# Layer scale on one core: 32-row pieces in six shared slots, all loads queued ahead of all stores on the two hardware rings

## The chip, the cores and the metric

One Trainium2 chip (trn2), one core. The time is device microseconds of one execution; the span is the time from the first to the last instruction in its profile. "Before" ran at 123.72 us (median of 3, from 123.56 to 123.85). I call a difference real only where several rounds and their interval show it.

## The reference

```python
B, S, D = 1024, 16, 512          # x, y: (B, S, D) bf16, gamma: (D,) bf16
def reference(x, y, gamma):
    return x + gamma * y
```

Two inputs and one output of 16.78 MB each must cross between DRAM and SBUF: 50.33 MB in all. There is one multiply and one add per element, and no reuse.

## The kernel before

The 16,384 rows of 512 elements are dealt to 128 partitions, so each partition owns 128 consecutive rows, 128 KB. A "piece" of n rows is n KB per partition; one transfer moves it for all partitions.

```python
MAIN_CHUNK = 16
TAIL_CHUNKS = [8, 8]
X_BUFS = 5
Y_BUFS = 6
# ... chunks = seven pieces of 16 rows, then 8 and 8
# ... pad_sb: unused bytes, so that the tiles begin at a multiple of 16,384 bytes
x_pool = ctx.enter_context(tc.tile_pool(name="xio", bufs=X_BUFS))
y_pool = ctx.enter_context(tc.tile_pool(name="yio", bufs=Y_BUFS))
# ... gamma is spread over the partitions by a matmul with a row of ones
r0 = 0
for cs in chunks:
    xt = x_pool.tile([P, max_chunk, D], xf.dtype, tag="xt")
    yt = y_pool.tile([P, max_chunk, D], yf.dtype, tag="yt")
    nc.sync.dma_start(out=xt[:, :cs, :], in_=xv[:, r0 : r0 + cs, :])      # hardware ring of SP
    nc.scalar.dma_start(out=yt[:, :cs, :], in_=yv[:, r0 : r0 + cs, :])    # hardware ring of ACT
    nc.vector.tensor_tensor(out=yt, in0=yt, in1=gamma_sb[:, None, :].to_broadcast(...), op=mult)  # cut
    nc.vector.tensor_tensor(out=yt, in0=xt, in1=yt, op=add)                                       # cut
    nc.gpsimd.dma_start(out=ov[:, r0 : r0 + cs, :], in_=yt[:, :cs, :])    # software queue of POOL
    r0 += cs
```

Stores are issued as soon as a piece is added, so they run beside the loads of later pieces.

## Time and profile before

| | before |
|---|---|
| time, median | 123.72 us |
| span of the profiled execution | 122.05 us |
| VectorE busy | 71.1 us, 58% |
| bytes | 33.56 MB read, 16.78 MB written |
| first DMA packet starts, last one ends | 1.73 us, 120.47 us |

The page of the kernel before, cut to the rows that matter: busy time by engine, then the span in 40 slices (busy tenths of VectorE and of the 16 DMA engines, and what they moved), then the DMA queues (q1 is SP's ring and carries x, q10 is ACT's and carries y, q0 is the software queue of POOL and carries the stores).

```profile
span 122.0 us, 123 instructions
...
PE 0.6 (0%) x1; PEld 0.1 (0%) x1; DVE 71.1 (58%) x21; POOL 5.6 (5%) x14
...
DVE  0010799780019999950079995940019999859600
...
DMA  4999999999999999999999999999999999999993
GB/s 118 424 435 430 430 430 430 430 349 435 430 430 435 435 440 430 430 430 430 430 440 435 430 430 430 430 430 430 430 397 454 413 430 419 464 430 430 397 427 126
...
q10 hardware_dynamic: 1296, 16.78, 32.7%
q1 hardware_dynamic: 1296, 16.78, 32.7%
q0 software_dynamic: 1328, 16.78, 32.2%
```

The DMA row is 9 in all but the first and last slice, and each of the three queues takes a third of the engines' time. The kernel is bound by the DMA engines; the zeros of VectorE cost nothing. One slice, near 26 us, moved only 349 GB/s although the engines were busy in it.

The groups of instructions of the same profile (busy us and mean ns of one, then the idle time before them and what ended it):

```profile
L94 DVE TENSOR_TENSOR yt<-yt,gamma_sb 128x8192 bf16<-128x8192 bf16 (+1 forms) x9 | 35.5, 3949 | 35.5 <-DMA yt<-in_y_dram 35.5
L100 DVE TENSOR_TENSOR yt<-xt,yt 128x8192 bf16<-128x8192 bf16 (+1 forms) x9 | 35.2, 3944 | 0.0
```

The last part of its timeline (start us, us, engine, line, operation):

```profile
108.26 2.29 DVE L94 TENSOR_TENSOR yt<-yt,gamma_sb 128x4096 bf16<-128x4096 bf16 x1 [2.02 <-DMA yt<-in_y_dram]
110.47 4.49 DVE L100 TENSOR_TENSOR yt<-xt,yt 128x4096 bf16<-128x4096 bf16 x2
113.05 0.53 POOL L106 DMA_DIRECT2D out_dram<-yt  x1 [8.18 <-DVE yt L100]
115.25 0.53 POOL L106 DMA_DIRECT2D out_dram<-yt  x1 [1.67 <-DVE yt L100]
```

The last y lands at 108.2 us. After that come two short multiplies, two short adds and two 1 MB stores; the 8-row tail is there so that this end is short.

 16 KB in 611 ns on 16 engines is 429 GB/s. The Trainium skill, page "DMA: Bandwidth & Descriptors", section "Where 436 GB/s comes from", puts the ceiling of the ports at 435 GB/s for the 16 engines; the trace agrees to 1.5%, so nothing that leaves the bytes alone can win more than a little. The same section says that for transfers between HBM and SBUF a limit of about 358 GB/s per core binds; the 429 GB/s here, with one core at work, lie above it, so here the measurement decides.

### The profile page before, as it was taken

How to read it: one execution, taken by the hardware profiler on the slowest of the kernel's cores; microseconds unless marked ns; L12 is line 12 of the kernel's file. 1: busy time of each engine (PE TensorE's matmuls, PEld its weight loads, DVE VectorE, ACT ScalarE, POOL GpSimd, SP SyncE). 2: the span in 40 equal slices, each digit the busy share in tenths (PEclk: the TensorE clock that was granted, in tenths of full speed). 3: DMA queues.
4: the chain of work that ended last, by engine and by line, in shares of the span. 5: the costliest groups of instructions: out<-in, count | busy, mean ns of one | idle time of the engine just before them, and what ended most of it. 6: DMA issues, size and time to landing. Idle time of an engine off the chain costs nothing.

```text
span 122.0 us, 123 instructions
## 1 busy us (share of the span) xinstructions
PE 0.6 (0%) x1; PEld 0.1 (0%) x1; DVE 71.1 (58%) x21; POOL 5.6 (5%) x14
## 2 busy tenths in 40 slices
PE   0010000000000000000000000000000000000000
PEld 0000000000000000000000000000000000000000
DVE  0010799780019999950079995940019999859600
POOL 2000000100000010100000011000000010100300
DMA  4999999999999999999999999999999999999993
GB/s 118 424 435 430 430 430 430 430 349 435 430 430 435 435 440 430 430 430 430 430 440 435 430 430 430 430 430 430 430 397 454 413 430 419 464 430 430 397 427 126
DMA packets 3920, 50.33 MB, mean 412 GB/s; under 512 B 464, under 2 KB 464, under 8 KB 464
## 3 DMA queue, kind: packets, MB, share of 16 engines
q10 hardware_dynamic: 1296, 16.78, 32.7%
q1 hardware_dynamic: 1296, 16.78, 32.7%
q0 software_dynamic: 1328, 16.78, 32.2%
HBM read 33.56 MB, written 16.78 MB: 412 GB/s over the span
## 4 chain that ended last, share of the span: by engine, by line
DMA 66%; issue 15%; DVE 11%; POOL 1%; POOLq 0%; DVEq 0%; ACTq 0%
DMA yt<-in_y_dram 50%; DMA out_dram<-yt 16%; DVE yt L100 7%; DVE yt L94 4%; POOL out_dram L106 1%; POOLq L134 0%; DVEq L94 0%; POOLq L106 0%; ACTq L93 0%; DVEq L100 0%
## 5 line engine op out<-in xcount | busy, mean ns | idle before, releaser
L94 DVE TENSOR_TENSOR yt<-yt,gamma_sb 128x8192 bf16<-128x8192 bf16 (+1 forms) x9 | 35.5, 3949 | 35.5 <-DMA yt<-in_y_dram 35.5
L100 DVE TENSOR_TENSOR yt<-xt,yt 128x8192 bf16<-128x8192 bf16 (+1 forms) x9 | 35.2, 3944 | 0.0
L106 POOL DMA_DIRECT2D out_dram<-yt x9 | 4.8, 533 | 109.1 <-DVE yt L100 109.1
L86 DVE CAST gamma_sb<-gamma_ps 128x512 bf16<-128x512 f32 x1 | 0.7, 690 | 7.5 <-PE gamma_ps L85 7.5
L80 POOL DMA_DIRECT2D gamma_row<-in_gamma_dram x1 | 0.6, 618 | 0.8 <-POOLq L123 0.8
L81 DVE MEMSET ones_row<- 1x128 bf16 x1 | 0.2, 165 | 0.8 <-PEq L123 0.8
L85 PE MATMUL gamma_ps<-gamma_row,ones_row 1*128 1x512 bf16 x1 | 0.6, 577 | 7.9 <-DMA gamma_row<-in_gamma_dram 7.9
L123 POOL MEMSET const-float32-0.0<- 128x1 f32 x1 | 0.1, 98 | 0.2 <-issue 0.2
L123 POOL MEMSET const-bfloat16-1.0<- 128x1 bf16 x1 | 0.1, 102 | 0.0
L85 PEld LDWEIGHTS <-ones_row 1*128 1x128 bf16 x1 | 0.1, 101 | 1.0 <-DVE pad_sb L83 1.0
L123 POOL MEMSET const-float32-1.0<- 128x1 f32 x1 | 0.1, 98 | 0.0
L123 POOL MEMSET const-uint8-127<- 128x1 uint8 x1 | 0.1, 98 | 0.0
L83 DVE MEMSET pad_sb<- 128x16 uint32 x1 | 0.1, 72 | 0.0
## 6 DMA issues: line engine op xcount, KB each, us to landing
yt<-in_y_dram ACTq DMA_DIRECT2D x7, 2048.0 KB, 45.5
xt<-in_x_dram SPq DMA_DIRECT2D x7, 2048.0 KB, 45.4
out_dram<-yt POOLq DMA_DIRECT2D x7, 2048.0 KB, 19.1
xt<-in_x_dram SPq DMA_DIRECT2D x2, 1024.0 KB, 44.4
yt<-in_y_dram ACTq DMA_DIRECT2D x2, 1024.0 KB, 32.7
out_dram<-yt POOLq DMA_DIRECT2D x2, 1024.0 KB, 5.5
gamma_row<-in_gamma_dram POOLq DMA_DIRECT2D x1, 1.0 KB, 6.6
```

The lines of the kernel that those rows point to most:

```text
L80: nc.gpsimd.dma_start(out=gamma_row[:], in_=gamma.unsqueeze(0))
L81: nc.vector.memset(ones_row[:], 1.0)
L83: nc.vector.memset(pad_sb[:, 0:64], 0)
L85: nc.tensor.matmul(gamma_ps[:], ones_row[:], gamma_row[:], start=True, stop=True)
L86: nc.vector.tensor_copy(out=gamma_sb[:], in_=gamma_ps[:])
L94: nc.vector.tensor_tensor(out=yt[:, :cs, :], in0=yt[:, :cs, :], in1=gamma_sb[:, None, :].to_broadcast([P, cs, D]), op=mybir.AluOpType.mult,)
L100: nc.vector.tensor_tensor(out=yt[:, :cs, :], in0=xt[:, :cs, :], in1=yt[:, :cs, :], op=mybir.AluOpType.add,)
L106: nc.gpsimd.dma_start(out=ov[:, r0 : r0 + cs, :], in_=yt[:, :cs, :])
L123: nc = _bacc.Bacc("TRN2", target_bir_lowering=False, num_devices=1)
```

## The change

The intent: longer transfers (half as many packets), no software queue in the way, and no store that delays a load. The schedule is fixed by hand, in program order. The diff, cut to its core (gone with it: the tail, the pad, the two pools):

```diff
-MAIN_CHUNK = 16
-TAIL_CHUNKS = [8, 8]
-X_BUFS = 5
-Y_BUFS = 6
+PIECE = 32
+SLOTS = 6
 ...
+    io_pool = ctx.enter_context(tc.tile_pool(name="io", bufs=SLOTS))
+    xs, ys = [], []
+    ctx.enter_context(tc.manual_schedule())
+    for c in range(n_pieces):                      # 4 pieces
+        r = slice(c * PIECE, (c + 1) * PIECE)
+        xt = io_pool.tile([P, PIECE, D], dt, tag="io")
+        yt = io_pool.tile([P, PIECE, D], dt, tag="io")
+        nc.sync.dma_start(out=xt[:], in_=xv[:, r, :])
+        nc.scalar.dma_start(out=yt[:], in_=yv[:, r, :])
         nc.vector.tensor_tensor(... mult ...)
         nc.vector.tensor_tensor(... add ...)
-        nc.gpsimd.dma_start(out=ov[:, r0 : r0 + cs, :], in_=yt[:, :cs, :])
+        xs.append(xt)
+        ys.append(yt)
+    for c in range(n_pieces):
+        r = slice(c * PIECE, (c + 1) * PIECE)
+        eng = nc.sync if c % 2 == 0 else nc.scalar
+        eng.dma_start(out=ov[:, r, :], in_=ys[c][:])
```

Eight tiles share six slots. In the built program x3 takes the slot of x0 (it waits for the first add) and y3 that of x1 (it waits for the second).

More of the change, by code (lines that the diff above doesn't have):

```diff
@@ L6 @@
 from concourse._compat import with_exitstack
-MAIN_CHUNK = 16
-TAIL_CHUNKS = [8, 8]
-X_BUFS = 5
-Y_BUFS = 6
-SBUF_ALIGN = 16384
-SLOT_ROUND = 32
-def _chunk_schedule(n_per_part: int) -> list[int]:
-    tail = [c for c in TAIL_CHUNKS if c < MAIN_CHUNK]
-    rem = n_per_part - sum(tail)
-    if rem < 0:
-        return [1] * n_per_part
-    chunks = []
-    while rem >= MAIN_CHUNK:
-        chunks.append(MAIN_CHUNK)
-        rem -= MAIN_CHUNK
-    if rem > 0:
-        chunks.append(rem)
-    chunks.extend(tail)
-    assert sum(chunks) == n_per_part, (chunks, n_per_part)
-    return chunks
-def _round_up(v: int, m: int) -> int:
-    return ((v + m - 1) // m) * m
+PIECE = 32
+SLOTS = 6
 @with_exitstack
@@ L51 @@
     N, D = xf.shape
-    assert N % P == 0, (N, P)
-    n_per_part = N // P
-    gdt = gamma.dtype
+    rows = N // P
+    n_pieces = rows // PIECE
+    dt = xf.dtype
     xv = xf.rearrange("(p n) d -> p n d", p=P)
@@ L58 @@
     ov = of.rearrange("(p n) d -> p n d", p=P)
-    chunks = _chunk_schedule(n_per_part)
-    max_chunk = max(chunks)
     const_pool = ctx.enter_context(tc.tile_pool(name="const", bufs=1))
-    gamma_row = const_pool.tile([1, D], gdt)
-    ones_row = const_pool.tile([1, P], gdt)
-    gamma_sb = const_pool.tile([P, D], gdt)
-    used = nc.sbuf_base
-    used = _round_up(used, SLOT_ROUND)
-    for nbytes in (D * mybir.dt.size(gdt), P * mybir.dt.size(gdt), D * mybir.dt.size(gdt)):
-        used += _round_up(nbytes, SLOT_ROUND)
-    pad_bytes = (-used) % SBUF_ALIGN
-    pad_sb = None
-    if pad_bytes > 0:
-        pad_sb = const_pool.tile([P, pad_bytes], mybir.dt.uint8)
-    x_pool = ctx.enter_context(tc.tile_pool(name="xio", bufs=X_BUFS))
-    y_pool = ctx.enter_context(tc.tile_pool(name="yio", bufs=Y_BUFS))
+    gamma_row = const_pool.tile([1, D], dt)
+    ones_row = const_pool.tile([1, P], dt)
+    gamma_sb = const_pool.tile([P, D], dt)
     psum_pool = ctx.enter_context(tc.tile_pool(name="psum", bufs=1, space=bass.MemoryType.PSUM))
@@ L81 @@
     nc.vector.memset(ones_row[:], 1.0)
-    if pad_sb is not None:
-        nc.vector.memset(pad_sb[:, 0:64], 0)
     gamma_ps = psum_pool.tile([P, D], mybir.dt.float32)
@@ L86 @@
     nc.vector.tensor_copy(out=gamma_sb[:], in_=gamma_ps[:])
-    r0 = 0
-    for cs in chunks:
-        xt = x_pool.tile([P, max_chunk, D], xf.dtype, tag="xt")
-        yt = y_pool.tile([P, max_chunk, D], yf.dtype, tag="yt")
-        nc.sync.dma_start(out=xt[:, :cs, :], in_=xv[:, r0 : r0 + cs, :])
-        nc.scalar.dma_start(out=yt[:, :cs, :], in_=yv[:, r0 : r0 + cs, :])
+    io_pool = ctx.enter_context(tc.tile_pool(name="io", bufs=SLOTS))
[7 more added lines that the diff above has]
+        nc.scalar.dma_start(out=yt[:], in_=yv[:, r, :])
         nc.vector.tensor_tensor(
-            out=yt[:, :cs, :],
-            in0=yt[:, :cs, :],
-            in1=gamma_sb[:, None, :].to_broadcast([P, cs, D]),
+            out=yt[:],
+            in0=yt[:],
+            in1=gamma_sb[:, None, :].to_broadcast([P, PIECE, D]),
             op=mybir.AluOpType.mult,
         )
-        nc.vector.tensor_tensor(
-            out=yt[:, :cs, :],
-            in0=xt[:, :cs, :],
-            in1=yt[:, :cs, :],
-            op=mybir.AluOpType.add,
-        )
-        nc.gpsimd.dma_start(out=ov[:, r0 : r0 + cs, :], in_=yt[:, :cs, :])
-        r0 += cs
-    assert r0 == n_per_part
+        nc.vector.tensor_tensor(out=yt[:], in0=xt[:], in1=yt[:], op=mybir.AluOpType.add)
+        xs.append(xt)
[4 more added lines that the diff above has]
+        eng.dma_start(out=ov[:, r, :], in_=ys[c][:])
 _INS = ['x', 'y', 'gamma']
```

## The prediction

> What bounds it now. 50.33 MB move (the page: 33.56 read, 16.78 written) and the 16 DMA engines are never free: the row of DMA busy tenths is 9 in every slice but the first and last, at 430 to 435 GB/s in most. VectorE is 58% busy and waits 35.5 us for y (groups by line): off the critical path. In the packet records a 16 KB packet takes 611 ns and an 8 KB packet 309, load or store, mixed or alone: 604 ns of data per 16 KB and 7 fixed, 429 GB/s on 16 engines, close to the 435 GB/s ceiling in the Trainium skill, "DMA: Bandwidth & Descriptors", section "Where 436 GB/s comes from". Between the first packet (1.73 us) and the end of the last (120.47) the mean engine is without one for 0.62 us. Each engine has 168 long and 48 short data packets, 117.5 us, and 28 completion packets of 9 ns. So of the span of 122.05 us, 1.7 are start, 117.7 packets, about 1.0 slow packets (one slice falls to 349 GB/s), skew and gaps, 1.6 the end.
>
> What the change does. Bytes stay. Packets become longer: at 32 KB 96 per engine x 1215 ns (estimate, 2 x 604 + 7) = 116.6 us; if still cut at 16 KB, 192 x 611 = 117.3. Completion packets: 13. Stores leave the software queue, whose stores land with up to 1.4 us between the first and last of 16 engines; the first eight hardware loads show 0.5 or less. The pad goes: tiles begin at byte 18,816, not a multiple of 256.
>
> Does an engine run dry? VectorE from its two shapes: 151 ns + 0.5215 per element, so 8.70 us at 16,384, 17.45 a pair. x0, y0 land near 22.6 us (second pair of before: 22.7), later pairs 19.4 apart: 42, 61.5, 81. Adds end near 40, 59.5, 79, 98.5. In the built program x3 waits for the first add and y3 for the second, so both are queued by 59.5, before x2 and y2 end at 61. Stores 0 and 1 run 80 to 100; store 2 is queued at 79, store 3 at 98.5, 1.5 us before it is wanted; the other ring would fill a short gap. VectorE stays hidden, with about 2 us of slack, and the first add at 40 instead of 22 us costs nothing because loads fill that time.
>
> Sum: start 1.7 + packets 116.7 to 117.4 + residue 0.5 + end 1.5 = 120.4 to 121.1 us of span, 1.0 to 1.6 less; the timed run is 1.67 above the span: 122.1 to 122.8. I say 122.4.
>
> Right if: DMA tenths stay 9; loads to 80 us, then stores alone near 430 GB/s; VectorE 70 us busy, TENSOR_TENSOR near 8.7; x3, y3 issued near 40 and 59.5; last landing near 119.5; stores' landing spread about 0.5.
>
> Wrong if: 40 us of stores alone run slower than the 12 us of them at the end of before (over 124); tiles off 256-byte alignment cost DMA beats (same page, "How a descriptor splits into AXI transactions": an unaligned start fetches unused bytes; I take under 1%, no run shows it yet); the slack is lost and both rings go empty; the end shrinks more than I think (towards 121).
>
> Chances: faster by over 2% 0.08, within 2% 0.85, slower by over 2% 0.07. Range 121.5 to 123.7.

## More of the kernel before

The trace also has a record of every DMA packet (start, duration, size, queue). A packet here is what one partition contributes to one transfer. Durations are remarkably constant:

```
packet      median duration     in which kernel
 8 KB         309 ns            before (tail)
16 KB         611 ns            before, loads and stores alike
32 KB        1213 ns            after, loads and stores alike
```

So a packet costs 301 to 302 ns per 8 KB plus 7 to 9 ns that do not depend on its size.

## The result, and the profile after

| | before | after |
|---|---|---|
| median | 123.67 us (4 runs, 123.56 to 123.85) | 123.22 us (4 runs, 123.17 to 123.34) |
| ratio | | 0.9964, 95% interval 0.995 to 0.9978 |

A ratio is the mean time of one kernel's fast runs over that of the other's fast runs in the same rounds, so it is not quite the ratio of the medians that stand beside it. A second set of five rounds (after_again below) gave 0.9966. The change is real and small: 0.45 us, where I had announced 1.3.

The page of the changed kernel, the same rows:

```profile
span 121.5 us, 80 instructions
...
PE 0.6 (0%) x1; PEld 0.1 (0%) x1; DVE 70.4 (58%) x10; POOL 0.8 (1%) x5
...
DVE  0002000499999399999679999907999990000000
...
DMA  5899999999999999999999999989898989898992
GB/s 173 378 486 389 475 399 464 399 464 421 442 432 432 410 453 410 453 399 464 410 453 410 453 410 453 345 345 518 356 507 356 507 356 507 367 496 389 475 410 108
...
q10 hardware_dynamic: 864, 25.17, 48.7%
q1 hardware_dynamic: 864, 25.17, 48.6%
q0 software_dynamic: 32, 0.00, 0.0%
```

Bytes and packets are counted in the slice in which a packet starts. With packets of 1.2 us in slices of 3 us the numbers swing (345, then 518): two neighbours have to be averaged. The pair 345, 345 near 77 us does not average out; that is a true loss.

Its groups and the timeline of its VectorE and rings:

```profile
L58 DVE TENSOR_TENSOR yt<-yt,gamma_sb 128x16384 bf16<-128x16384 bf16 x4 | 34.8, 8692 | 18.9 <-DMA yt<-in_y_dram 18.9
L64 DVE TENSOR_TENSOR yt<-xt,yt 128x16384 bf16<-128x16384 bf16 x4 | 34.8, 8692 | 0.1
```

```profile
0.74 59.20 ACTq L57 DMA_DIRECT2D yt<-in_y_dram  x4
0.74 39.83 SPq L56 DMA_DIRECT2D xt<-in_x_dram  x4
...
22.80 8.69 DVE L58 TENSOR_TENSOR yt<-yt,gamma_sb 128x16384 bf16<-128x16384 bf16 x1 [11.05 <-DMA yt<-in_y_dram]
31.52 8.69 DVE L64 TENSOR_TENSOR yt<-xt,yt 128x16384 bf16<-128x16384 bf16 x1
40.61 38.78 SPq L70 DMA_DIRECT2D out_dram<-yt  x2
...
82.85 8.69 DVE L58 TENSOR_TENSOR yt<-yt,gamma_sb 128x16384 bf16<-128x16384 bf16 x1 [3.83 <-DMA yt<-in_y_dram]
91.57 8.69 DVE L64 TENSOR_TENSOR yt<-xt,yt 128x16384 bf16<-128x16384 bf16 x1
```

The first add ends at 40.2 us, the last load lands at 82.8 us instead of 108.2, the last add ends at 100.3 us, and from there VectorE has nothing to do while 20 us of stores are still queued. The schedule is the one predicted, to within 2 us.

Here is where the loss can be seen without packet records. Stretches of both kernels: their length, then busy us of the engines, the granted clock, the mean busy share of the DMA engines (which can pass 1, as a packet counts where it starts), and GB/s. First before, then after:

```profile
20.00:30.00 10.00, 0.00 (x0) 0.00 (x0) 6.37 (x2) 0.55 (x1) 1.00 1.01 408
30.00:75.00 45.00, 0.00 (x0) 0.00 (x0) 30.52 (x7) 1.59 (x3) 1.00 1.01 431
75.00:82.00 7.00, 0.00 (x0) 0.00 (x0) 4.43 (x1) 0.53 (x1) 1.00 0.98 419
```

```profile
20.00:30.00 10.00, 0.00 (x0) 0.00 (x0) 7.20 (x1) 0.00 (x0) 1.00 0.97 419
30.00:75.00 45.00, 0.00 (x0) 0.00 (x0) 40.93 (x6) 0.00 (x0) 1.00 1.00 431
75.00:82.00 7.00, 0.00 (x0) 0.00 (x0) 4.02 (x1) 0.00 (x0) 1.00 0.99 379
```

Two things are to be seen. In the long middle both kernels move 431 GB/s: the packets twice as long do not show. And after, between 75 and 82 us, the engines are as busy as ever (0.99) and move only 379 GB/s. Before has its slow stretch earlier (408 from 20 to 30 us).

### One sum for all kernels

From the packet records the time between the start of the first packet and the end of the last (the window) can be split without remainder:

window = nominal + slow + idle - overlap,

all in us per DMA engine. *Nominal* gives every packet the median duration of its size. *Slow* is what packets took beyond that. *Idle* is the time with fewer than 16 packets in flight, *overlap* that with more than 16 (an engine then has two packets in flight, and a part of one hides behind the other). A transfer has *landed* when all 16 engines have reported their part of it.

| | window | nominal | slow | idle | overlap | last landing to end | span |
|---|---|---|---|---|---|---|---|
| before | 118.74 | 117.74 | 1.26 | 0.62 | 0.89 | 1.23 | 122.05 |
| after | 118.20 | 116.58 | 1.55 | 0.44 | 0.37 | 1.14 | 121.45 |
| after_again | 118.24 | 116.58 | 1.51 | 0.54 | 0.38 | 1.15 | 121.48 |
| half_packets | 118.72 | 117.55 | 1.47 | 0.51 | 0.81 | 0.88 | 121.70 |
| pieces16 | 118.28 | 117.55 | 1.12 | 0.40 | 0.79 | 0.89 | 121.45 |
| before_no_tail | 119.22 | 117.55 | 1.40 | 1.09 | 0.82 | 1.18 | 122.47 |

(The first packet starts at 1.73 to 1.77 us in all of them; 0.34 to 0.52 us pass between the last packet's end and its landing. One line is one execution. Nominal and overlap follow the number of packets and repeat to 0.01 us between after and after_again; slow and idle scatter, so differences of 0.2 us in them mean little.) The change did remove 1.16 us of nominal packet time. It gave back 0.52 of overlap and 0.29 of slow packets, and won 0.18 of idle time: 0.54 us of window.

All but 0.05 us (before) and 0.18 us (after) of the slow time lies in two places. In the first 5 us each engine's first packet takes longer, up to 2.07 us instead of 1.21 in the changed kernel: 0.59 us per engine are lost before, 0.60 after. The second place comes just ahead of the first store, in packets of loads. Start, end, queue, ns and bytes of four of the 16 packets concerned, all of them y3 loads, and last the first packet of store 0:

```
77.636 79.650 q10 2014 32768
77.637 79.691 q10 2054 32768
77.677 79.670 q10 1993 32768
77.696 79.663 q10 1967 32768
...
80.767 81.980 q1 1213 32768
```

### The profile page after: what moved, and what is told of

Its sections match the earlier page's. It is cut to its first block, busy times and chain, and to the rows that moved or that the text cites. A ratio compares the mean times of both kernels' runs of the same rounds, so it can differ in the third digit from the quotient of the medians.

```text
span 121.5 us, 80 instructions
## 1 busy us (share of the span) xinstructions
PE 0.6 (0%) x1; PEld 0.1 (0%) x1; DVE 70.4 (58%) x10; POOL 0.8 (1%) x5
## 3 DMA queue, kind: packets, MB, share of 16 engines
q10 hardware_dynamic: 864, 25.17, 48.7%
q1 hardware_dynamic: 864, 25.17, 48.6%
## 4 chain that ended last, share of the span: by engine, by line
DMA 53%; DVE 29%; ACTq 0%; issue 0%
DMA yt<-in_y_dram 53%; DVE yt L58 14%; DVE yt L64 14%; ACTq L57 0%
## 5 line engine op out<-in xcount | busy, mean ns | idle before, releaser
L58 DVE TENSOR_TENSOR yt<-yt,gamma_sb 128x16384 bf16<-128x16384 bf16 x4 | 34.8, 8692 | 18.9 <-DMA yt<-in_y_dram 18.9
L64 DVE TENSOR_TENSOR yt<-xt,yt 128x16384 bf16<-128x16384 bf16 x4 | 34.8, 8692 | 0.1
```

The lines of the kernel that those rows point to most:

```text
L58: nc.vector.tensor_tensor(out=yt[:], in0=yt[:], in1=gamma_sb[:, None, :].to_broadcast([P, PIECE, D]), op=mybir.AluOpType.mult,)
L64: nc.vector.tensor_tensor(out=yt[:], in0=xt[:], in1=yt[:], op=mybir.AluOpType.add)
```

## The experiments

Theories at the start. **P**: as predicted, packets are paid one after the other, each with its fixed few ns, and the rest is the software queue's. **O**: half of the fixed part was already hidden by overlap, which I put down to packets of two queues. **W** (A in the expectations): the loss ahead of the first store is a one-time cost of an engine's first write, to this output (A1) or at all (A2). All kernels gave the reference's result.

| run | median us | ratio to before | 95% interval |
|---|---|---|---|
| warm_out | 123.29 | 0.9956 | 0.9939 to 0.9972 |
| warm_scratch | 123.28 | 0.9962 | 0.9947 to 0.9978 |
| half_packets | 123.28 | 0.9959 | 0.9944 to 0.9975 |
| tail_split | 123.29 | 0.9961 | 0.9948 to 0.9975 |
| before_last_hw | 123.68 | 1.000 | 0.9988 to 1.0013 |
| last_sw | 123.25 | 0.9965 | 0.9952 to 0.9977 |
| pieces16 | 123.21 | 0.9954 | 0.9939 to 0.9968 |
| after_again | 123.31 | 0.9966 | 0.9953 to 0.9979 |
| before_no_tail | 124.22 | 1.0038 | 1.0026 to 1.0051 |
| pieces16_sw | 127.84 | 1.0335 | 1.032 to 1.0349 |
| hw_mixed | 133.98 | 1.0834 | 1.082 to 1.0849 |
| sw_stores | 134.50 | 1.0897 | 1.0851 to 1.0943 |

### Packet length: half_packets and pieces16

half_packets, on the changed kernel:

```diff
-        nc.sync.dma_start(out=xt[:], in_=xv[:, r, :])
-        nc.scalar.dma_start(out=yt[:], in_=yv[:, r, :])
+        for h in range(2):
+            k = slice(h * PIECE // 2, (h + 1) * PIECE // 2)
+            rh = slice(c * PIECE + k.start, c * PIECE + k.stop)
+            nc.sync.dma_start(out=xt[:, k, :], in_=xv[:, rh, :])
+            nc.scalar.dma_start(out=yt[:, k, :], in_=yv[:, rh, :])
# and each store in two halves likewise
```

> Same slots, same VectorE work, but every 32-row piece moved by two 16-row transfers, so packets of 16 KB. As predicted (7 ns fixed per packet, all of it serial) it costs 96 x 9 = 0.9 us more and 0.1 us of completion packets: ratio to before near 1.004. Rival (neighbouring packets of two queues overlap by 3 or 4 ns, so only half of the fixed part is paid): about 0.5 us, less 0.15 us won at the end by the finer packets: ratio near 0.999.

Measured: 123.28 us, ratio 0.9959. Nominal rose by 0.97 us, as both theories said; overlap rose from 0.37 to 0.81, so the window rose by 0.52 only, as O said. O had the size right and the reason wrong: overlap does not need two queues. In hw_mixed and in sw_stores, two runs below, the last store runs alone, 128 packets on one queue, and they overlap by about 3 ns each all the same; over whole profiles it is 3.3 to 3.8 ns per packet, in all 17. So some 5 ns of the fixed part are really paid per packet (0.52 us of window for 108 more packets per engine, completion packets counted). The time did not rise at all, so O's ratio near 0.999 missed too. P is out: 32 KB packets are worth 0.5 us of window at most, and here not even that reached the time, because the end after the last landing was 0.26 us shorter, and because the profiled execution was the slowest of its six (123.46 us). That end is a row of waits of SyncE, one semaphore after the other, some 0.06 us each: in the changed kernel the last store's semaphore is the first of five in the row, here it is the last.

This run bears on the alignment too. Its tiles begin at byte 18,816, and its 16 KB packets, loads and stores, have the same median of 611 ns as those of before, whose tiles begin at multiples of 16 KB. The Trainium skill, "DMA: Bandwidth & Descriptors", section "How a descriptor splits into AXI transactions", has extra beats for a descriptor that does not start at a multiple of 256 bytes; for packets of this length no run here shows any cost.

pieces16:

```diff
-PIECE = 32
-SLOTS = 6
+PIECE = 16
+SLOTS = 12
```

> The changed kernel with 16-row pieces in twelve slots (the same bytes of SBUF), order and rings kept. By the prediction's packet term it is 0.9 us slower than the changed kernel (ratio 1.004). By what the run with half packets showed (0.97 us more of nominal packets, but 0.45 us more overlap between packets) and with the last semaphores on other places, ratio 0.995 to 0.998, that is, no difference to the changed kernel that these rounds can show.

Measured: 123.21 us, ratio 0.9954, the same as the changed kernel within the intervals. Two independent edits say it: the large piece is not what wins. Nothing that I tried beats the changed kernel by a margin that these rounds show; pieces16 equals it with finer pieces.

### The loss ahead of the first store: four runs with an early write

warm_out and warm_scratch, ahead of everything else, in program order:

```diff
+    warm = const_pool.tile([P, 256], dt)
+    nc.vector.memset(warm[:], 0.0)
+    nc.sync.dma_start(out=ov[:, rows - 1, 0:256], in_=warm[:])     # warm_scratch: another DRAM tensor
```

> A 64 KB store of zeros into the last row of every partition of the output goes first on the SP ring, ahead of x0 (the last real store overwrites it). Theory A (the first write of a DMA engine to this output stalls the engine once, about 0.75 us, seen before the first stores at 77 to 80 us): that stall is gone from the packets at 77 to 80 us, it falls into the start where the engines already lose about 0.75 us, so ratio to before about 0.991 (122.6 us) if the two overlap, and the same as the changed kernel (0.996) if they add up. Theory C (the stall comes from the ring turning from loads to stores, or from the late phase): packets at 77 to 80 us still take about 2000 ns, ratio 0.996 to 0.999.

> The same small store, but into another DRAM tensor. Theory A1 (the stall belongs to the first write to the output's own addresses): packets at 77 to 80 us still take about 2000 ns and the ratio is that of the changed kernel or a little worse, 0.996 to 0.999. Theory A2 (it belongs to an engine's first write of any kind to DRAM): the stall is gone as with the store into the output, same time as that run.

Measured: 0.9956 and 0.9962. The small store left no mark of its own (its packets, from 4.8 to 12.6 us, took 27 ns each), and the long packets were there all the same, 0.78 and 0.88 us per engine ahead of the first large store. The output's own addresses are out (A1, by warm_out), and so is a first write of any size (A2, by both).

big_mid_scratch and big_mid_out put a store of 1 MB (8 KB per partition) behind x0 on SP's ring, into another tensor or into the output:

> A store of 8 KB per partition (1 MB, zeros) into another DRAM tensor stands behind x0 on the SP ring, so it runs near 22 us. Theory: an engine's first full-size write costs it some 0.6 to 0.9 us once; then packets near 20 to 22 us are long and those near 77 to 80 us are not. Rival 1 (it belongs to the output tensor): none at 22, long ones at 77 to 80. Rival 2 (it belongs to the change from loads to stores on a ring each time it happens after a pause): long ones at both places. The time is 2.4 us worse by the bytes and says nothing.

> The same 1 MB store, into the last 8 rows of each partition of the output (overwritten by the last real store). Rival 1 above expects long packets near 20 to 22 us and none at 77 to 80; the first-write theory expects the same as in the run with the other tensor; rival 2 long ones at both places.

Measured: both tensors alike, so the loss does not belong to the output's addresses. Long packets stood at both places: 0.30 and 0.35 us per engine ahead of the early store at 22 us, 0.45 and 0.33 us ahead of the first real one at 82. Together that is about what one first store costs. That is what rival 2 announced, but half as large at each place, and the kernel before speaks against a price for every turn: its second store is issued at 45.2 us, after the first landed at 41.4, and no packet between 35 and 100 us took over 150 ns more than the median of its size.

x_first loads x0 and x1 first and y0, y1 after them:

```diff
+            ring = nc.sync if c == 0 else nc.scalar      # pieces 0 and 1 only
+            ring.dma_start(out=xt[:], in_=xv[:, r, :])
+            ring.dma_start(out=yt[:], in_=yv[:, r, :])
```

> x0 and x1 are loaded first, one on each ring, then y0 and y1, so y is first touched near 22 us. If each engine pays for its first touch of each tensor, packets near 20 to 22 us take some 700 ns longer than 1213. If it pays only for its first read at all, no packet there is long and the loss stays at the start. The time itself will be worse (the first multiply waits until 42 us) and says nothing.

Measured: no long packet near 22 us, so y is not paid for when it is first touched; the loss at the start is one of the first packets as such. Ahead of the first store (72 us) 1.24 us were lost, and another 0.53 us near 61 us, where ACT's ring ran empty. I have no explanation for the latter.

The second loss follows the first large store wherever that stands. Nine of the profiles (the rest lost 0.33 to 0.93, x_first 1.24):

```
first store packet, us    us per engine lost in the 4.5 us ahead of it
before            27.2    0.62
pieces16_sw       27.3    0.67
before_no_tail    27.4    0.81
sw_stores         46.8    0.90
hw_mixed          61.6    0.82
half_packets      79.2    0.55
after_again       79.4    0.73
pieces16          80.7    0.30
after             80.8    0.77
```

That it goes with the first store phase, in either kernel, on either kind of queue, is shown. Its size is not fixed (pieces16 lost 0.30). What the engine does in that time is not; it stays open.

### Which ring: before_last_hw, last_sw, sw_stores

before_last_hw changes only the ring of the two tail stores of the kernel before; last_sw only that of the last store of the changed kernel:

```diff
-        nc.gpsimd.dma_start(out=ov[:, r0 : r0 + cs, :], in_=yt[:, :cs, :])
+        eng = nc.gpsimd if cs == MAIN_CHUNK else nc.sync if r0 == n_per_part - 16 else nc.scalar
+        eng.dma_start(out=ov[:, r0 : r0 + cs, :], in_=yt[:, :cs, :])
```

```diff
-        eng = nc.sync if c % 2 == 0 else nc.scalar
+        eng = nc.gpsimd if c == n_pieces - 1 else nc.sync if c % 2 == 0 else nc.scalar
```

> The kernel before with nothing changed but the ring of its two last 8-row stores: SP and ACT instead of the software queue. Theory (what the change really won lies behind the last landing: POOL's drain of the software queue, 0.25 us, and the look at the semaphores): span down by 0.2 to 0.4 us, ratio 0.997 to 0.998, packets' window unchanged at 118.7. If instead the change won by its packets or by the queue order, ratio 1.000 here.

> The changed kernel with only its last store moved to the software queue. Same theory: 0.25 to 0.3 us come back, all of it after the last landing (1.14 to about 1.4 us), ratio to before 0.998 to 0.999. Otherwise 0.996.

Measured: 1.000 and 0.9965. I had read a software queue's clean-up of 0.25 us from two traces and made a theory of it; in the time it does not exist, in either direction. That theory fell.

sw_stores puts all four stores of the changed kernel back on the software queue:

```diff
-        eng = nc.sync if c % 2 == 0 else nc.scalar
-        eng.dma_start(out=ov[:, r, :], in_=ys[c][:])
+        nc.gpsimd.dma_start(out=ov[:, r, :], in_=ys[c][:])
```

> The changed kernel with its four stores issued on the software queue again (they then run beside the loads, and y3 waits for the first store). If leaving the software queue is what the change really won, the whole gain goes back: ratio to before 0.999 to 1.001. If the software queue costs only its clean-up behind the last landing (0.25 us read from the two traces: the drain on POOL ended 0.45 us after the last landing), ratio near 0.998 to 0.999. If the queue does not matter, 0.996 as the changed kernel. The long packets before the first store should again be there, now near 40 us.

Measured: 134.5 us. A miss of all three branches: I had thought about the ring and forgotten the order. Stores on a ring of their own run beside the loads, and in this build y3 also waits for the first store. The next run takes that apart.

### The order: hw_mixed, before_no_tail, pieces16_sw

hw_mixed keeps rings and slots, and puts stores 0 and 1 ahead of x3 and y3:

```diff
 ... cut: the six slots are named so that x3 and y3 keep theirs; the last loop begins at store 2
+        if c == 3:
+            nc.sync.dma_start(out=ov[:, 0:PIECE, :], in_=ys[0][:])
+            nc.scalar.dma_start(out=ov[:, PIECE : 2 * PIECE, :], in_=ys[1][:])
         nc.sync.dma_start(out=xt[:], in_=xv[:, r, :])
         nc.scalar.dma_start(out=yt[:], in_=yv[:, r, :])
```

> The changed kernel with the same slots and rings, but stores 0 and 1 put ahead of the loads x3 and y3 on their rings. Estimate from the traces: stores 0 and 1 run 61 to 81 us, x3 and y3 land near 101 instead of 81 to 83, the last add ends near 118.5 instead of 100.3, the engines run dry from about 110 us, and the last store of 4 MB takes 10 us after that: 129 to 131 us of span, ratio 1.06 to 1.08. If order does not matter (the engines are busy anyway), 0.996.

Measured: 133.98 us, ratio 1.0834, a little over the estimate. The end of its timeline, and three stretches of it (columns as above):

```profile
102.45 8.69 DVE L62 TENSOR_TENSOR s<-s,gamma_sb 128x16384 bf16<-128x16384 bf16 x1 [22.56 <-DMA s<-in_y_dram]
111.18 8.69 DVE L68 TENSOR_TENSOR s<-s,s 128x16384 bf16<-128x16384 bf16 x1
119.90 0.35 ACTq L74 DMA_DIRECT2D out_dram<-s  x1
```

```profile
100.00:110.00 10.00, 0.00 (x0) 0.00 (x0) 7.54 (x1) 0.00 (x0) 1.00 0.97 419
110.00:120.00 10.00, 0.00 (x0) 0.00 (x0) 9.84 (x2) 0.00 (x0) 1.00 0.00 0
120.00:133.00 13.00, 0.00 (x0) 0.00 (x0) 0.00 (x0) 0.00 (x0) 1.00 0.75 323
```

From 110 to 120 us the DMA engines did nothing: every other store was done, and the last one waited for 17.4 us of VectorE. So the order of the queues is what makes 32-row pieces possible at all. The Trainium skill, "DMA: Bandwidth & Descriptors", section "Issuing engines are not separate DMA queues", says that transfers issued by different engines share the same 16 DMA engines and interleave, whoever issued them. The trace agrees (in the changed kernel two busy rings hold 48.7% and 48.6% of the engines), and the consequence is here: a store that is put in early takes its bytes from a load, and the load's lateness comes back at the end.

before_no_tail is the kernel before with TAIL_CHUNKS = [], eight equal pieces; pieces16_sw is pieces16 with its stores on the software queue (the edit of sw_stores):

> The kernel before with eight equal pieces of 16 rows, no 8-row tail. Theory: in its order, where stores run beside loads, the tail is what keeps the engines busy to the end; without it the last add ends near 117 us, with 1 to 3 us of idle engines: ratio 1.01 to 1.03, like pieces16_sw. If the tail only costs packets (8 KB ones, 0.2 us): ratio 0.998.

> 16-row pieces in twelve slots, with the stores on the software queue beside the loads. Theory: what matters at the end is when the last load lands; beside the stores it lands near 106 to 108 us instead of 82, the last multiply and add of 16 rows take 8.8 us, and the last 2 MB store then has the engines nearly to itself: engines idle 1 to 3 us near 117 us, ratio to before 1.01 to 1.03. If order and ring do not matter with small pieces: 0.996 to 1.000.

Measured: 1.0038 and 1.0335. Idle engines were the cause in both, as expected; the sizes differed from what I had expected of the first (0.85 us of idle from 115 to 120 us, not 1 to 3) and of the second (4.8 us in the whole window, 4.4 of it from 115 to 120 us). The rows of before_no_tail, then of pieces16_sw:

```profile
DMA  5999999999999999999999999999999999999694
GB/s 144 428 434 433 428 433 433 434 300 433 433 434 433 433 433 434 428 428 428 434 428 428 428 428 428 428 428 428 428 434 433 439 428 433 439 433 433 294 428 171
```

```profile
DMA  4999999999999999999999999999999999993193
GB/s 146 432 421 416 447 447 416 437 333 416 442 442 442 421 416 416 447 447 432 421 416 437 447 442 421 416 426 437 452 426 421 416 437 458 432 421 166 83 416 166
```

The hole before the last store is the 294 of the first and the 166, 83 of the second; the changed kernel has none. With eight equal pieces the old order takes 124.22 us and the new one 123.21: the new order is worth about 1.0 us, if rings and slots, which differ too, are worth nothing. But the kernel before is not that kernel. Its 8-row tail had already won 0.4 of it (124.22 to 123.78 in the same rounds), at the price of some 8 KB packets (0.20 us of nominal time).

### The tail of the changed kernel: tail_split, and a repetition

```diff
+        parts = [16, 8, 8] if c >= n_pieces - 2 else [PIECE]     # rows per store
```

> Stores 2 and 3 are cut into 16, 8 and 8 rows, nothing else. Theory: 0.25 us of the window is lost because the engines end up to one 1213 ns packet apart, and 0.3 us because the last store's semaphore is the first of five that SyncE then looks at; with short last packets and the last store on the last semaphore both shrink: packets' window 118.2 to about 118.1, end after the last landing 1.14 to about 0.9, ratio to before 0.993 to 0.994. Rival: the tail is not what limits, ratio 0.996 as the changed kernel.

Measured: 0.9961. Window 118.38 and end 0.89 us: the end shrank as expected, the window did not, as the short packets cost 0.29 us of nominal time. Nothing is left in the time.

> The changed kernel unchanged, a second time: ratio to before 0.996, loss before the first store again 0.6 to 0.9 us if it belongs to 32 KB packets, 0.3 to 0.5 if the sizes seen so far were only scatter from profile to profile.

Measured: 0.9966, loss ahead of the first store 0.73 us. So 0.77 was no accident of one profile for this kernel. It does not follow that it belongs to 32 KB packets: before_no_tail lost 0.81 us with 16 KB ones.

## Why the prediction was right or wrong

**Right.** The kernel is bound by the DMA engines before and after. VectorE stays hidden: 8.69 us per instruction (8.70 predicted), adds ending at 40.2, 59.6, 79.0 and 100.3 us (40, 59.5, 79, 98.5). Packets go out at 32 KB and take 1213 ns (1215). Stores alone, 37 us of them, run no slower than mixed traffic (435 GB/s from 82 to 100 us, as before in the same stretch). Tiles that do not begin at a multiple of 256 bytes showed no cost (611 ns for 16 KB packets either way). The time stayed within 2%. Not right were the last landing (120.31 us, not 119.5, for the reason below) and the landing spread of the stores, the time between the first and the last of the 16 engines: 0.5 us as predicted for three of them, 1.71 for the other.

**The slack.** It was lost on one ring, as feared, and cost nothing. y3 was issued at 59.6 us and its first packet started at 63.06, after ACT's ring had run dry at 60.9; SP's ring filled the gap, y3 landed at 82.8 instead of 81, and no engine went idle.

**Wrong: the size of the gain**, 0.45 us instead of 1.3. The step that failed is the term "residue 0.5" of the sum "start 1.7 + packets 116.7 to 117.4 + residue 0.5 + end 1.5". With 32 KB packets that sum was 120.4 us. Measured: start 1.76, packets 116.58, residue 1.62, end 1.50, together 121.45. The residue is 1.1 us too small, and the other terms hold. It failed for two reasons:

1. I took "about 1.0 slow packets, skew and gaps" of before as something that the software queue causes and that would halve without it. Its parts were 0.59 us of long first packets, 0.62 us ahead of the first store, and 0.62 us of idle, less 0.89 of overlap. The first two have nothing to do with that queue: they stand in the changed kernel as 0.60 and 0.77, and in every kernel here, on either kind of ring. Nor is the skew a mark of it, which the prediction read from stores that land with up to 1.4 us between the engines: in after_again, with all stores on hardware rings, the four spreads are 0.65 to 1.86 us.
2. I subtracted the fixed part of the saved packets in full. Before, 0.89 us of it were already hidden by overlap; after, 0.37 are. half_packets shows the term alone: 0.97 us of nominal packets became 0.52 us of window and nothing in the time. In sum: 0.50 that did not halve, 0.52 of overlap lost, 0.29 more of slow packets, less 0.18 of idle, give the 1.1 us.

A small third one: I took 1.67 us from span to timed run from a single pair. Over the timed runs it is about 1.77.

**What the 0.45 us come from is only bounded, not settled.** They are not the packet length (half_packets and pieces16 keep them), not the ring of the last stores (before_last_hw and last_sw do not move), not the alignment. They are there in every kernel of the table of runs that queues loads first on the hardware rings, and in none that lets stores run beside the loads. Order and kind of queue are not separated for them: no run keeps the old order and its short tail with all stores on hardware rings. The closest that the runs come: loads first make the tail unnecessary, and without its short packets the old kernel would not have kept the engines busy to the end. Splitting 0.45 us further would need differences of 0.1 us, and single executions of one kernel differ by 0.3 to 0.5.

## What to carry to other kernels

When DMA engines are busy all the time, write the bound as packets plus named losses, and do not promise a loss away before you know where in the trace it lies: a remainder of 1 us that looks like "skew" can be two fixed costs that every variant pays. A cost per packet read as median duration is an upper limit, since successive packets of an engine overlap (here by 3 to 4 ns). Queue the loads ahead of the stores where the last piece's compute is long: stores put in early delay the last load, and with 32-row pieces that cost nearly 11 us; with small pieces and a short tail the old order lost only 0.45.

## What the Trainium skill lacked or had wrong

- Page "DMA: Bandwidth & Descriptors", section "Latency and other measured facts": the first-byte latency of a hardware ring is given as some 0.6 us. Counted from the end of the issuing instruction the first load agrees, with 0.63 us to its first packet (1.02 us from the start, 0.74 to 1.76 us). y3 does not: 3.45 us from the start (59.61 to 63.06 us) and 3.11 from the end, queued while the other ring kept the engines busy and its own ran dry. The page has no figure for that case.
- Same page: nothing on the first packets of a program. In the changed kernel the first 32 KB packet took 1.31 to 2.07 us instead of 1.21 on the 16 engines; in the mean 0.4 to 0.7 us per engine are lost so in all 16 kernels profiled.
- Same page: nothing on the loss ahead of the first large store, 0.3 to 0.9 us per engine in every kernel but x_first (1.24), not prevented by an earlier small store of 64 KB.
- Same page, section "Why small descriptors are slow (HBM only)": it has a fixed cost of about 3 cycles per packet. The durations of 8, 16 and 32 KB packets (309, 611, 1213 ns) leave 7 to 9 ns in the packet records, which are far longer than the 256-byte pieces of the page's example, so the two figures are not held against each other. No page has a figure for how far successive packets of one engine overlap: here 3.3 to 3.8 ns per packet (about 3 with one queue alone), 0.36 to 0.89 us per engine in all, which hides about half of it.
- The alignment cost of "How a descriptor splits into AXI transactions" is not seen at 16 KB: 611 ns aligned and unaligned.
